# A Performer attention and mixer kernel: the second channel product by one level of Strassen's algorithm

## The chip, the cores and the metric

The kernel runs on one core of a Trainium2 chip. The metric is the device time of one execution in microseconds (us). Five engines work side by side, each through its own ordered queue: TensorE (PE in the profile; PEld is its weight loads), VectorE (DVE), ScalarE (ACT), GpSimd (POOL) and SyncE (SP, which only issues transfers). An instruction that waits holds up all that is behind it in its queue. Matrix products go to PSUM, which has eight banks of 128 x 512 fp32 values; the other engines read them from there.

## The reference

Attention with random features (8 batches, 8 heads, 576 rows, 64 columns), then one layer of an MLP mixer over the result `x` (8 x 576 x 512):

```python
q_p, k_p = (phi(q_s), phi(k_s))          # 128 features, exp
kv = np.einsum('bhsm,bhsd->bhmd', k_p, v)
num = np.einsum('bhsm,bhmd->bhsd', q_p, kv)
return (num / den)                       # becomes x, heads side by side
...
h = np.maximum(xt @ w_tok1, 0.0) @ w_tok2     # token mix, xt = x transposed
u = x + h.transpose(0, 2, 1)
h2 = np.maximum(u @ w_ch1, 0.0) @ w_ch2       # 512 -> 1536 -> 512
return (u + h2)
```

`u @ w_ch1` is the first channel product, the one with `w_ch2` the second. Inputs are fp32; the kernel computes its products in fp16 and sums in fp32.

## The kernel before

Each batch's 576 rows are split into 512 main rows and 64 tail rows. A batch goes through these stages, named by their functions:

- `attention`: per pair of heads, the feature products (L638, L652) and their exponentials on ScalarE (L514), a maximum and its reciprocal on VectorE (L664, L666), the scaling of v on GpSimd (L671), the kv product (L684), the numerators (L720, L722) and their division on VectorE (L729, L730).
- `token_mix` (`token_mix_first` for batch 0): the two token products (L759, L776), a relu between them, of whose two blocks one is on ScalarE (L765) and one on VectorE (L767), the addition that makes `u` (L779), and a transposing transfer of `u` to `uT` on SP's queue.
- `token_tail`: the tail rows of two batches at a time (L835, L841), collected as a ninth "batch" of 512 rows.
- `channel_mix(c, ...)`, for c = 0 to 7 and for c = 8, the tail rows. The first channel product (L854) makes twelve blocks of 128 channels by 512 rows, four matmuls of 512 columns each; a relu (L874, on ScalarE for batches from 2 on and all of batch 1) writes each to its place in `r3`, [128, 12, 512] fp16. The second product (L892) works through four row blocks j of 128 rows: for each, twelve matmuls with `r3`'s block as the stationary operand and `wc2[:, cb]` (512 columns) as the moving one accumulate in one bank; VectorE adds `u` and writes fp32 to `o` (L901; L898 for batch 0), and a store of 256 KB goes out from SP. `r3` has two buffers, `o` four, the PSUM banks are one ring of eight.

The order of the work isn't written by hand. Every helper registers jobs by `add` (L59): an engine, a planned cost in us, a key, what it depends on, and which ring places it takes and gives. The planner's `run` then puts them in order: for each engine it finds the jobs that can start first, with margins for work handed over between engines (0.3 us ahead of TensorE), and among those the one with the lowest key (L123, L124):

```python
first = min(r[0] for r in ready)
t, _, j = min((r for r in ready if r[0] <= first + 1e-6), key=lambda r: r[1])
```

So the order on every queue is settled when the kernel is built, from planned costs; on the chip each engine follows it and waits by semaphores. Transfers from GpSimd's queue keep the order in which they were registered. Keys come from the batch number and the tables `KEYS`, `NEAR` and `HEAD`; `BY` says which engine does some of the evacuations. Between its early jobs TensorE gets idle matmuls (L943) until the first large product.

Of the kernel before, what the change touches and what calls it, by code (L numbers as in the profile page):

```python
# [9 lines left out]
FP32 = mybir.dt.float32  # L10
FP16 = mybir.dt.float16
# [5 lines left out]
KEYS = {"a": -1.349, "as": 0.099, "t": -1.509, "ts": 0.187, "gv": 2.165, "lt": -2.428, "lv": -3.989, "to": -2.341, "tt": 0.635, "ks": 1.094, "km": 0.303, "vs": -0.113, "l1": -0.452, "kt": -0.062}  # L17
NEAR = {"1": {"a": -1.734, "as": 0.259, "t": -2.775, "ts": 0.45, "gv": -0.056, "km": -2.03, "vs": -0.397, "kt": 0.253}, "2": {"a": -2.686, "as": 0.0, "t": -0.603, "ts": 0.324, "gv": -1.313, "km": 3.931, "vs": 0.571, "lv": -3.347, "lt": -2.872, "kt": -0.122}}
HEAD = {"kp": [-3.838, -3.822, -3.881, -3.404], "ke": [-2.728, -2.927, -2.827, -2.727], "km": [-4.039, -3.592, -4.221, -2.25], "vs": [-3.448, -3.487, -3.196, -2.472], "qp": [-3.203, -3.403, -3.303, -3.488], "qe": [-3.328, -3.374, -2.153, -3.748], "kv": [-3.407, -3.257, -2.676, -3.133], "ko": [-2.32, -3.035, -3.463, -3.168], "n": [-3.199, -3.47, -3.182, -2.377, -2.999, -3.268, -2.999, -2.899], "no": [-4.124, -3.487, -3.919, -3.144, -3.226, -3.426, -3.126, -2.386], "ktm": -3.643, "kt": -4.584, "kte": -5.022, "qt": -3.759, "qte": -5.587, "kx": [-6.213, -5.658, -5.326, -5.458], "kxo": [-6.855, -7.05, -5.723, -4.783], "ktx": -5.661, "ktxo": -5.912, "qx": [-4.987, -3.488], "qxo": [-4.073, -2.977], "qtx": -4.584, "qtxo": -3.371, "t1": [0.229, -1.008, -0.737, -0.359], "re": [0.072, -0.781, 0.181, -0.024], "ut": [0.056, -0.48, -0.104, -0.341], "uo": [-0.099, -0.259, -0.108, 0.38], "vbd": -8.41, "w1": -9.7, "w1t": -9.38, "w2t": -9.78, "wa": -8.03, "wb": -9.17, "w2": -10.08}
BY = {"kx": "ADDD", "ktx": "A", "qx": "DD", "qtx": "A", "ko": "DADD", "re": "AAAA", "uo": "AADD", "no": "DDADDADD", "r0": "AAAAADAAADAA", "ko1": "DDAA", "r1": "AAAAAAAAAAAA"}  # L20
# [17 lines left out]
class Planner:  # L38
# [20 lines left out]
    def add(self, eng, cost, key, fn, deps=(), take=(), give=(), rows=False, wire=0.0):  # L59
        job = Job(eng, cost, key, fn, [d for d in deps if d is not None], list(take), list(give), rows, wire)  # L60
        for g in job.give:
            self.left[g] = self.left.get(g, 0) + 1
        self.jobs.append(job)
        return job
# [113 lines left out]
def kernel(  # L178
# [37 lines left out]
    def sb(shape, dt, name):  # L216
        return pool.tile(shape, dt, name=name)

    def ring(n, shape, dt, name):
        return [sb(shape, dt, f"{name}{i}") for i in range(n)]  # L220

    COUNT = {"qT": 3, "kT": 3, "v": 3, "vt": 2, "qp": 4, "kp": 4, "vs": 4, "qpt": 2, "kpt": 2, "vbd": 2,
             "kvsb": 3, "ktt": 2, "x": 3, "r1": 3, "u": 3, "uT": 3, "r3": 2, "o": 4, "bank": 8}
# [4 lines left out]
    omega_nat = sb([P, D], FP32, "omega_nat")  # L228
    omega16 = sb([P, 2 * D], FP16, "omega16")
    omT = sb([P, M], FP16, "omT")  # L230
    ident32 = sb([P, P], FP32, "ident32")
    ident16 = sb([P, P], FP16, "ident16")
    junk = sb([P, B], FP16, "junk")
    zeros = sb([P, SM], FP16, "zeros")
# [26 lines left out]
    t_o = ring(COUNT["o"], [P, DM], FP32, "o")  # L261
# [30 lines left out]
    def mm(n, cols):  # L292
        return n * (cols / 2400.0 + 0.0025)
# [167 lines left out]


# [289 lines left out]
    def token_mix(b, key, step, jx):  # L752
        jr = []
        for tb in range(NT):
# [7 lines left out]
            def relu(tb=tb, n=n):  # L762
                o = t_r1[place("r1", b)][:, tb, :]
                if tb == 0:
                    nc.scalar.activation(out=o, in_=bank(n), func=AF.Relu)  # L765
                else:
                    nc.vector.tensor_relu(out=o, in_=bank(n))  # L767
            jr.append(add("ACT" if tb == 0 else "DVE", 0.5 if tb == 0 else 0.69, key + step * tb * 0.2, relu, deps=[j1],
# [75 lines left out]

    def channel_mix(c, key, jt):
        def moving(db):
            return (t_uT[place("uT", c)] if c < B else uTt)[:, :, db, :]
        jr = []
        for cb in range(NCB):
# [16 lines left out]
            else:  # L866
                j1 = add("PE", mm(4, 512), key + 0.5 * cb / NCB, c1, deps=[*jt, j_wc1[cb // (NCB // 2)], *first], take=[("bank", n), ("r3", c)],
# [9 lines left out]
            jr.append(add("ACT" if on_act else "DVE", 0.5 if on_act else 0.69, key + 0.5 * cb / NCB, relu, deps=[j1], take=[("r3", c)], give=[("bank", n)]))  # L877
        for j in range(NJ):
            last = c == B and j == NJ - 1
            for hf in range(2 if last else 1):  # L880
# [15 lines left out]
                def oadd(j=j, n=n, cols=cols):  # L896
                    if c == 0:
                        nc.vector.tensor_copy(out=t_o[place("o", (c, j))], in_=bank(n))  # L898
                        return
                    uu = t_u[place("u", c)][:, j, :] if c < B else ut[j]  # L900
                    nc.vector.tensor_tensor(out=t_o[place("o", (c, j))][:, cols], in0=uu[:, cols], in1=bank(n)[:, cols], op=ALU.add)  # L901
                jo = add("DVE", (0.55, 0.27)[hf] if last else 0.69, k2, oadd, deps=[prev], take=[("o", (c, j))], give=[("bank", n)] + ([("u", c)] if 0 < c < B else []))
                def store(j=j, cols=cols, last=last):
                    o = t_o[place("o", (c, j))]
# [7 lines left out]
                dma("SP", k2, 0.65, store, deps=[jo], give=[("o", (c, j))], cost=0.4 if c < B else 0.8)  # L912
# [63 lines left out]
```

## Time and profile before

| | |
|---|---|
| median of 3 runs | 289.49 us (289.16 to 290.48) |
| profiled execution: span from first to last instruction | 287.0 us |
| profiled execution: its own time | not given beside the span; the median lies 2.5 us over the span |
| TensorE busy, mean granted clock | 280.2 us, 0.998 |
| second channel product (L892), 444 matmuls | 100.7 us |
| first channel product (L854), 424 matmuls | 99.2 us (88.7 for c below 8, 10.5 for the tail rows) |
| VectorE / ScalarE / GpSimd busy | 152.6 / 153.6 / 93.7 us |
| bytes moved by transfers | 39.59 MB, 138 GB/s on the mean |

A busy time is the union of an engine's instructions. A matmul's listed duration reaches from its start to the end of its drain, so that of two in a row overlap; the distance from start to start (the pitch) is what one costs in a stream. In a group, the number after the bar is busy us, then the mean ns of one instruction, then the idle time of the engine ahead of them with what ended it. A timeline line has start, length, engine, line, operation, tiles, shape and count.

### The profile page before, as it was taken

To read this page: it belongs to the slowest core of one execution; us is meant where nothing else is said; L and a number is where in the kernel's file an instruction comes from. 1 tells how busy PE (TensorE), PEld (TensorE's weight loads), DVE (VectorE), ACT (ScalarE), POOL (GpSimd) and SP (SyncE) were. 2 spreads that over 40 slices of the span, in tenths; PEclk is the share of its full clock that TensorE was granted. 3 is DMA by queue.
4 is the path that set the end of the run, shared out by engine and by line. 5 is a ranking of instruction groups with operands and counts; after the bars stand their busy time and mean duration, and the time that the engine had idled before them with its cause. 6 is when DMAs were issued, how large, how long until landed. Compare 5 with 4: busy or idle time off the path is not lost.

```text
span 287.0 us, 5605 instructions
## 1 busy us (share of the span) xinstructions
PE 280.2 (98%) x2186; PEld 141.6 (49%) x2186; DVE 152.6 (53%) x330; ACT 153.6 (54%) x322; POOL 93.7 (33%) x126
## 2 busy tenths in 40 slices
PE   8999999999999999999999999999999999999994
PEld 4585554445544544454445544454455444444442
DVE  3986954546669624745584647564686331031012
ACT  2984872098449552875286537753576402602600
POOL 8994950157015701480166016601141000000000
PEclk9999999999999999999999999999999999999999
DMA  8999999999975995999989967996531042013013
GB/s 191 197 191 195 202 216 143 214 196 190 166 110 149 136 175 117 202 168 198 111 156 206 201 85 144 199 189 95 129 75 39 0 110 110 2 48 116 2 45 102
DMA packets 85721, 39.59 MB, mean 138 GB/s; under 512 B 64384, under 2 KB 80128, under 8 KB 85504
## 3 DMA queue, kind: packets, MB, share of 16 engines
q0 software_dynamic: 34288, 17.45, 44.4%
q1 hardware_dynamic: 50624, 21.01, 33.2%
q10 hardware_dynamic: 784, 0.79, 0.8%
q8 instruction: 17, 0.28, 0.4%
q14 instruction: 8, 0.07, 0.1%
HBM read 35.88 MB, written 16.52 MB: 183 GB/s over the span
## 4 chain that ended last, share of the span: by engine, by line
PE 90%; POOL 5%; DMA 3%; issue 1%; ACT 0%; DVE 0%; POOLq 0%; DVEq 0%
PE bank L892 33%; PE bank L854 32%; PE bank L776 4%; PE bank L759 4%; DMA r<-in_k_dram 3%; PE bank L638 3%; PE bank L652 3%; PE bank L684 2%; PE bank L720 2%; POOL vs L671 1%; PE bank L760 1%; POOL r L313 1%; PE bank L835 1%; PE bank L485 1%; PE bank L722 1%
## 5 line engine op out<-in xcount | busy, mean ns | idle before, releaser
L892 PE MATMUL bank<-wc,r 128*128 128x512 f16 (+2 forms) x444 | 100.7, 374 | 0.0
L874 ACT ACTIVATE r<-bank 128x512 f16<-128x512 f32 x106 | 62.7, 606 | 64.5 <-PE bank L854 64.4
L854 PE MATMUL bank<-uT,wc 128*128 128x512 f16 x376 | 88.7, 379 | 0.0
L892 PEld LDWEIGHTS <-r 128*128 128x128 f16 x444 | 40.9, 98 | 48.9 <-issue 4.4
L854 PEld LDWEIGHTS <-wc 128*128 128x128 f16 x424 | 39.7, 98 | 43.1 <-issue 0.4
L514 ACT ACTIVATE qp<-bank 128x512 f16<-128x512 f32 x64 | 35.8, 646 | 13.0 <-PE bank L652 13.0
L664 DVE TENSOR_REDUCE km<-kp 128x8 f16<-128x1024 f16 x32 | 38.5, 1202 | 2.3 <-ACT kp L514 2.3
L514 ACT ACTIVATE kp<-bank 128x512 f16<-128x512 f32 x64 | 34.6, 630 | 6.6 <-PE bank L638 6.4
L671 POOL TENSOR_TENSOR vs<-v,vs 128x512 f16<-128x512 f16 x32 | 33.3, 1063 | 13.8 <-DVE vs L666 4.3
L901 DVE TENSOR_TENSOR o<-u,bank 128x512 f32<-128x512 f16 x28 | 19.1, 683 | 34.5 <-PE bank L892 34.4
L730 DVE TENSOR_TENSOR x<-bank,rc 128x320 f16<-128x320 f32 x62 | 30.5, 492 | 2.1
L779 DVE TENSOR_TENSOR u<-x,bank 128x512 f16<-128x512 f16 x28 | 17.4, 683 | 9.5 <-PE bank L776 9.5
L729 DVE RECIPROCAL rc<-bank 128x5 f32<-128x5 f32 x62 | 11.5, 186 | 16.0 <-PE bank L722 15.8
L596 POOL TENSOR_TENSOR vbd<-vt,vbd 128x512 f16<-128x512 f16 (+1 forms) x7 | 8.2, 1173 | 35.0 <-PE bank L835 14.8
L380 POOL COPY junk<-kT 128x1 f16<-128x1 f16 x6 | 1.1, 186 | 50.5 <-DMA kT<-k 50.5
L767 DVE TENSOR_SCALAR r<-bank 128x512 f16<-128x512 f32 x7 | 4.8, 692 | 21.1 <-PE bank L760 21.1
L759 PE MATMUL bank<-x,w1m 128*128 128x512 f16 x56 | 14.4, 379 | 0.0
L720 PEld LDWEIGHTS <-qp 128*128 128x128 f16 x256 | 12.3, 98 | 4.0
L684 PEld LDWEIGHTS <-kp 128*128 128x128 f16 x256 | 11.1, 98 | 5.7 <-issue 1.1
L684 PE MATMUL bank<-vs,kp 128*128 128x65 f16 x256 | 12.9, 194 | 0.7 <-ACT r L874 0.7
L720 PE MATMUL bank<-kvsb,qp 128*128 128x65 f16 x256 | 13.5, 194 | 0.0
L776 PE MATMUL bank<-r,w 128*128 128x512 f16 x56 | 13.4, 380 | 0.0
(109 smaller groups left out, 269.5 us busy)
## 6 DMA issues: line engine op xcount, KB each, us to landing
out_dram<-o SPq DMA_DIRECT2D x32, 256.0 KB, 2.7
q<-in_q_dram POOLq DMA_DIRECT2D x6, 576.0 KB, 6.8
wc<-in_moe_w_ch_dram POOLq DMA_DIRECT2D x4, 768.0 KB, 10.6
k<-in_k_dram POOLq DMA_DIRECT2D x6, 512.0 KB, 9.1
v<-in_v_dram POOLq DMA_DIRECT2D x6, 512.0 KB, 6.7
r<-in_q_dram POOLq DMA_DIRECT2D x4, 256.0 KB, 7.2
v<-in_v_dram POOLq DMA_DIRECT2D x4, 256.0 KB, 7.1
out_dram<-o SPq DMA_DIRECT2D x5, 128.0 KB, 2.3
```

The costliest lines, as they stand in the source:

```text
L514: nc.scalar.activation(out=out, in_=in_, func=AF.Exp, bias=0.0, scale=1.0)
L664: nc.vector.reduce_max(out=mx, in_=kpv, axis=AX.X)
L671: nc.gpsimd.tensor_tensor(out=vs[:, :, 0:D], in0=t_v[place("v", b)][:, hh[0] : hh[0] + 2, :].rearrange("p h (j d) -> p (h j) d", d=D), in1 ...
L684: nc.tensor.matmul(ps[:, i, :], kpv[:, 2 * i + j // 2, j % 2, :], vs[:, i * NJ + j, 0 : D + 1], start=(i == 0 and j == 0), stop=False, ski ...
L720: nc.tensor.matmul(ps[:, k, j * 65 : (j + 1) * 65], st, s[:, i, 0 : D + 1], start=True, stop=True)
L730: nc.vector.tensor_tensor(out=t_x[place("x", b)][:, :, (2 * hp + hs[0]) * D : (2 * hp + hs[0] + n) * D].rearrange("p j (i d) -> p i j d", ...
L759: nc.tensor.matmul(ps, w1m[:, j, tb * P : (tb + 1) * P], x[:, j, :], start=(j == 0), stop=False)
L776: nc.tensor.matmul(ps, w2_of(tb, j), r1[:, tb, :], start=(tb == 0), stop=(tb == NT - 1))
L854: nc.tensor.matmul(ps, wc1[:, db, cb * P : (cb + 1) * P], moving(db), start=(db == 0), stop=(db == ND - 1))
L874: nc.scalar.activation(out=o, in_=bank(n), func=AF.Relu)
L892: nc.tensor.matmul(ps[:, cols], r3[:, cb, j * P : (j + 1) * P], wc2[:, cb, cols], start=(cb == 0), stop=(cb == NCB - 1))
L901: nc.vector.tensor_tensor(out=t_o[place("o", (c, j))][:, cols], in0=uu[:, cols], in1=bank(n)[:, cols], op=ALU.add)
```

## The change

The second channel product of batches 1 to 7 is computed by one level of Strassen's algorithm in Winograd's form. `r3` (512 rows x 1536 channels) and `wc2` (1536 x 512) are cut in halves both ways, and seven products of 256 rows x 768 channels x 256 columns take the place of eight. In detail:

- Four sums of `wc2`'s quarters (T1 to T4, [128, 6, 256] fp16 each) are made once, on VectorE.
- Per batch, four sums of `r3`'s quarters (S1, S2, S3 and one that overwrites the quarter r3(1,0)) are made on VectorE in fp16, each in two halves of 128 x 768 elements: eight instructions, one after the other within a half.
- Each of the seven products is twelve matmuls with a moving operand of 256 columns. Its [256 x 256] result is one bank. Four products accumulate in bank X, two in Z, one in Y. VectorE reads bank X after each of its four products, before the next one is added to it; with one reading of Y and two of Z that makes seven readings of 128 x 512 elements a batch into `o`, which then has two buffers of two row blocks. Two stores of 512 KB take the place of four of 256 KB.
- The product waits for all twelve relus of the batch. The blocks of the first channel product are made in the order 0, 6, 1, 7, and so on.
- The second token-mix relu goes from VectorE to ScalarE (`BY["re1"]`). All of the eight sums are on VectorE (`BY["S"]` is `DDDDDDDD`).
- Four small early tiles (`zeros`, `ident32`, `omega_nat`, `omega16`) lie in the memory of `S`.
- Every job's key comes from the table `TURN`, 1195 numbers in the order of registration, divided by 1000; `KEYS["ks"]`, by which two jobs with 64-row matmuls are favoured one after the other, goes from 1.094 to 2.577.

Batch 0 and the tail rows keep the old product. The diff, without the table's numbers and the lines of `KEYS` and `BY`:

```diff
+TURN = [
...
+]
...
     def add(self, eng, cost, key, fn, deps=(), take=(), give=(), rows=False, wire=0.0):
+        key = TURN[len(self.jobs)] / 1000.0 if TURN else key
...
-             "kvsb": 3, "ktt": 2, "x": 3, "r1": 3, "u": 3, "uT": 3, "r3": 2, "o": 4, "bank": 8}
+             "kvsb": 3, "ktt": 2, "x": 3, "r1": 3, "u": 3, "uT": 3, "r3": 2, "S": 1, "o": 2, "bank": 8}
...
     banks = [pspool.tile([P, 512], FP32, name=f"bank{i}") for i in range(COUNT["bank"])]
-    omega_nat = sb([P, D], FP32, "omega_nat")
-    omega16 = sb([P, 2 * D], FP16, "omega16")
+    NH = NCB // 2
+    DH = DM // 2
+    t_S = sb([P, 3, NH, 2 * P], FP16, "S")
+    t_T = sb([P, 4, NH, DH], FP16, "T")
+    early = t_S.rearrange("p a b c -> p (a b c)")
+    zeros = early[:, 0:SM]
+    ident32 = early[:, SM : SM + 2 * P].bitcast(FP32)
+    omega_nat = early[:, SM + 2 * P : SM + 2 * P + 2 * D].bitcast(FP32)
+    omega16 = early[:, SM + 2 * P + 2 * D : SM + 2 * P + 4 * D]
...
-    ident32 = sb([P, P], FP32, "ident32")
...
-    zeros = sb([P, SM], FP16, "zeros")
...
-    t_o = ring(COUNT["o"], [P, DM], FP32, "o")
+    t_o = ring(COUNT["o"], [P, 2, DM], FP32, "o")
...
+    W11, W12, W21, W22 = [wc2[:, NH * i : NH * i + NH, DH * e : DH * e + DH] for i in range(2) for e in range(2)]
+    T1, T2, T3, T4 = [t_T[:, i] for i in range(4)]
+    j_T = []
+    for out_, a, b in ((T1, W12, W11), (T2, W22, T1), (T3, W22, W12), (T4, W21, T2)):
+        j_T.append(add("DVE", 0.95, KEYS["T"], lambda o=out_, a=a, b=b: nc.vector.tensor_tensor(out=o, in0=a, in1=b, op=ALU.subtract), deps=[*j_wc2, *j_T[-1:]]))
...
             j1 = add("PE", mm(5, 512), key + step * tb * 0.2, t1, deps=[*jx, j_w1, j_w1t[b % 2]], take=[("bank", n), ("r1", b)])
...
-                if tb == 0:
+                if tb == 0 or BY["re1"] == "A":
                     nc.scalar.activation(out=o, in_=bank(n), func=AF.Relu)
...
-            jr.append(add("ACT" if tb == 0 else "DVE", 0.5 if tb == 0 else 0.69, key + step * tb * 0.2, relu, deps=[j1],
+            on_act = tb == 0 or BY["re1"] == "A"
+            jr.append(add("ACT" if on_act else "DVE", 0.5 if on_act else 0.69, key + step * tb * 0.2, relu, deps=[j1],
...
+    def channel_out_fast(c, key, jr):
+        def r3(i, e):
+            return t_r3[place("r3", c)][:, NH * e : NH * e + NH, 2 * P * i : 2 * P * i + 2 * P]
+        def S(i):
+            return t_S[:, i - 1]
+        sums = {}
+        for g in range(2):
+            part = slice(g * NH // 2, (g + 1) * NH // 2)
+            need = [jr[cb + NH * e] for cb in range(part.start, part.stop) for e in range(2)]
+            steps = (
+                (1, lambda: (S(1), r3(1, 0), r3(1, 1)), ALU.add),
+                (3, lambda: (r3(1, 0), r3(0, 0), r3(1, 0)), ALU.subtract),
+                (2, lambda: (S(2), S(1), r3(0, 0)), ALU.subtract),
+                (4, lambda: (S(3), r3(0, 1), S(2)), ALU.subtract),
+            )
+            prev = []
+            for k, (i, what, op) in enumerate(steps):
+                on_pool = BY["S"][4 * g + k] == "P"
+                def go(what=what, op=op, part=part, on_pool=on_pool):
+                    o, a, b = what()
+                    (nc.gpsimd if on_pool else nc.vector).tensor_tensor(out=o[:, part], in0=a[:, part], in1=b[:, part], op=op)
+                job = add("POOL" if on_pool else "DVE", 1.6 if on_pool else 0.5, key + KEYS["S"] + 0.1 * g + 0.01 * k, go, deps=[*need, *prev], take=[("S", c)])
+                prev = [job]
+                sums.setdefault(i, []).append(job)
+        last = sums[4]
+        ops = (
+            ("X", lambda: r3(0, 0), W11, []),
+            ("Y", lambda: r3(0, 1), W21, []),
+            ("X", lambda: S(2), T2, last),
+            ("Z", lambda: S(1), T1, last),
+            ("X", lambda: r3(1, 0), T3, last),
+            ("Z", lambda: S(3), W22, last),
+            ("X", lambda: r3(1, 1), T4, last),
+        )
+        ends = {"X": 6, "Y": 1, "Z": 5}
+        step = (1.0 - KEYS["c2"]) / 7
+        held = {}
+        def read(k, b, i, e, base, deps, free):
+            def go():
+                o = t_o[place("o", (c, i))][:, :, DH * e : DH * e + DH]
+                ps = bank((b, c)).rearrange("p (j d) -> p j d", j=2)
+                a = t_u[place("u", c)][:, 2 * i : 2 * i + 2, DH * e : DH * e + DH] if base else o
+                nc.vector.tensor_tensor(out=o, in0=a, in1=ps, op=ALU.add)
+            return add("DVE", 0.69, key + KEYS["c2"] + step * k, go, deps=deps, take=[("o", (c, i))],
+                       give=([("bank", (b, c))] if free else []) + ([("u", c)] if base else []))
+        done, outs = [], {}
+        for k, (b, a_of, w, need) in enumerate(ops):
+            def go(k=k, b=b, a_of=a_of, w=w):
+                ps, a = bank((b, c)), a_of()
+                for j in range(2):
+                    for cb in range(NH):
+                        nc.tensor.matmul(ps[:, j * DH : (j + 1) * DH], a[:, cb, j * P : (j + 1) * P], w[:, cb, :],
+                                         start=(b not in held and j == 0 and cb == 0), stop=False, skip_group_check=True)
+                held[b] = True
+            deps = [*need, *jr, *j_T, *j_wc2] + ([outs["sA"]] if k == 2 else [outs["s2"]] if k == 4 else [outs["22"]] if k == 5 else [outs["s3"]] if k == 6 else [])
+            j = add("PE", mm(2 * NH, DH), key + KEYS["c2"] + step * k, go, deps=deps, take=[("bank", (b, c))], give=[("r3", c)] + ([("S", c)] if need else []))
+            j.heavy = True
+            if k == 0:
+                outs["sA"] = read(k, "X", 0, 0, True, [j], False)
+            elif k == 1:
+                outs["11"] = read(k, "Y", 0, 0, False, [j, outs["sA"]], True)
+            elif k == 2:
+                outs["s2"] = read(k, "X", 0, 1, True, [j], False)
+            elif k == 3:
+                j_z = j
+            elif k == 4:
+                outs["s3"] = read(k, "X", 1, 1, True, [j], False)
+                outs["22"] = read(k + 0.1, "Z", 1, 1, False, [j_z, outs["s3"]], False)
+            elif k == 5:
+                outs["12"] = read(k, "Z", 0, 1, False, [j, outs["s2"]], True)
+            else:
+                outs["21"] = read(k, "X", 1, 0, True, [j], True)
+        for i, need in ((0, ["11", "12"]), (1, ["21", "22"])):
+            def store(i=i):
+                nc.sync.dma_start(out=out[c, 0:SM, :].rearrange("(p j) d -> p j d", j=NJ)[:, 2 * i : 2 * i + 2, :], in_=t_o[place("o", (c, i))])
+            dma("SP", key + 0.9 + 0.1 * i, 1.3, store, deps=[outs[x] for x in need], give=[("o", (c, i))], cost=0.4)
     def channel_mix(c, key, jt):
         def moving(db):
             return (t_uT[place("uT", c)] if c < B else uTt)[:, :, db, :]
-        jr = []
-        for cb in range(NCB):
+        jr = [None] * NCB
+        fast = NPE - 1 <= c < B
+        order = [x for i in range(NH) for x in (i, i + NH)] if fast else range(NCB)
+        for pos, cb in enumerate(order):
...
-                j1 = add("PE", mm(4, 512), key + 0.5 * cb / NCB, c1, deps=[*jt, j_wc1[cb // (NCB // 2)], *first], take=[("bank", n), ("r3", c)],
+                j1 = add("PE", mm(4, 512), key + 0.5 * pos / NCB, c1, deps=[*jt, j_wc1[cb // (NCB // 2)], *first], take=[("bank", n), ("r3", c)],
                        give=[("uT", c)] if c < B else [])
             j1.heavy = True
...
-            jr.append(add("ACT" if on_act else "DVE", 0.5 if on_act else 0.69, key + 0.5 * cb / NCB, relu, deps=[j1], take=[("r3", c)], give=[("bank", n)]))
+            jr[cb] = (add("ACT" if on_act else "DVE", 0.5 if on_act else 0.69, key + 0.5 * pos / NCB, relu, deps=[j1], take=[("r3", c)], give=[("bank", n)]))
+        if fast:
+            channel_out_fast(c, key, jr)
+            return
         for j in range(NJ):
...
                 k2 = key + 0.5 + 0.5 * (3 * j + 3) / 12
                 def oadd(j=j, n=n, cols=cols):
                     if c == 0:
-                        nc.vector.tensor_copy(out=t_o[place("o", (c, j))], in_=bank(n))
+                        nc.vector.tensor_copy(out=t_o[place("o", (c, j // 2))][:, j % 2], in_=bank(n))
                         return
                     uu = t_u[place("u", c)][:, j, :] if c < B else ut[j]
-                    nc.vector.tensor_tensor(out=t_o[place("o", (c, j))][:, cols], in0=uu[:, cols], in1=bank(n)[:, cols], op=ALU.add)
-                jo = add("DVE", (0.55, 0.27)[hf] if last else 0.69, k2, oadd, deps=[prev], take=[("o", (c, j))], give=[("bank", n)] + ([("u", c)] if 0 < c < B else []))
+                    nc.vector.tensor_tensor(out=t_o[place("o", (c, j // 2))][:, j % 2, cols], in0=uu[:, cols], in1=bank(n)[:, cols], op=ALU.add)
+                jo = add("DVE", (0.55, 0.27)[hf] if last else 0.69, k2, oadd, deps=[prev], take=[("o", (c, j // 2))], give=[("bank", n)] + ([("u", c)] if 0 < c < B else []))
                 def store(j=j, cols=cols, last=last):
-                    o = t_o[place("o", (c, j))]
+                    o = t_o[place("o", (c, j // 2))][:, j % 2]
...
-                dma("SP", k2, 0.65, store, deps=[jo], give=[("o", (c, j))], cost=0.4 if c < B else 0.8)
+                dma("SP", k2, 0.65, store, deps=[jo], give=[("o", (c, j // 2))], cost=0.4 if c < B else 0.8)
...
```

## The prediction

> **What bounds the kernel now.** I read the profile in this order: the page's busy table and its chain, a window that leaves out start and end, the timeline of TensorE, then that of the engines it hands to. The page first.
>
> ```profile
> span 287.0 us, 5605 instructions
> PE 280.2 (98%) x2186; PEld 141.6 (49%) x2186; DVE 152.6 (53%) x330; ACT 153.6 (54%) x322; POOL 93.7 (33%) x126
> PEclk9999999999999999999999999999999999999999
> PE 90%; POOL 5%; DMA 3%; issue 1%; ACT 0%; DVE 0%; POOLq 0%; DVEq 0%
> ```
>
> TensorE is the chain, at full granted clock. The window from 44 to 284 us, in the columns PE, PEld, DVE, ACT, POOL, then clock, DMA share and GB/s:
>
> ```profile
> 44.00:284.00 240.00, 238.90 (x1727) 116.05 (x1723) 120.86 (x247) 122.36 (x248) 58.94 (x78) 1.00 0.72 128
> ```
>
> 1.1 us of 240 is not PE, and that is what follows the last matmul at the end. So time is TensorE's instruction stream, added up. Its timeline gives the pitch (a listed length contains the last matmul's drain, so I use differences of starts):
>
> ```profile
> 20.26 0.39 PE L803 MATMUL bank<-x,w1m 128*128 128x128 f16 x4
> 20.49 0.22 PE L804 MATMUL bank<-x,w1t 128*128 128x128 f16 x1
> 20.54 0.39 PE L803 MATMUL bank<-x,w1m 128*128 128x128 f16 x4
> ...
> 230.24 10.52 PE L892 MATMUL bank<-wc,r 128*128 128x512 f16 x48
> 240.60 10.52 PE L854 MATMUL bank<-uT,wc 128*128 128x512 f16 x48
> 250.96 3.62 PE L892 MATMUL bank<-wc,r 128*128 128x512 f16 x16
> ```
>
> 48 matmuls of 512 columns take 10.36 us, 215.8 ns each; five of 128 columns take 0.28 us, 56 ns each, every one with its own weight load. Between them (215.8 - 56)/384 = 0.416 ns a column.
>
> The VectorE timeline at the end of a block, and the groups by shape:
>
> ```profile
> 233.03 0.69 DVE L901 TENSOR_TENSOR o<-u,bank 128x512 f32<-128x512 f16 x1 [2.27 <-PE bank L892]
> ...
> L671 POOL TENSOR_TENSOR vs<-v,vs 128x512 f16<-128x512 f16 x32 | 33.3, 1063 | 13.8 <-DVE vs L666 4.3 <-PE bank L722 3.6 <-PE bank L684 2.4
> L730 DVE TENSOR_TENSOR x<-bank,rc 128x320 f16<-128x320 f32 x62 | 30.5, 492 | 2.1
> L901 DVE TENSOR_TENSOR o<-u,bank 128x512 f32<-128x512 f16 x28 | 19.1, 683 | 34.5 <-PE bank L892 34.4
> L492 DVE COPY qT<-bank 128x1024 f16<-128x1024 f16 x4 | 2.6, 660 | 0.0
> L492 DVE CAST kT<-bank 128x512 f16<-128x512 f32 x3 | 2.0, 688 | 2.3 <-PE bank L485 2.2
> ```
>
> The first quarter of L892's 48 matmuls ends at 230.24 + 12 x 0.2158 = 232.83, and L901 begins at 233.03: 0.2 us from the last matmul to the reader, then 0.69 us of reading. VectorE is at 120.86/240 = 50%, and TensorE waits for it nowhere here.
>
> **The change, part by part.** *Products.* Batches 1 to 7 lose 48 matmuls of 512 columns each, 10.36 us. They get 7 products of 12 matmuls at 256 columns. That shape isn't in the trace, so I take the line between its neighbours: 56 + 128 x 0.416 = 109.3 ns, bounded by 107.9 (half of 215.8) and 112 (twice 56). 84 x 109.3 = 9.18 us. The gain is 1.18 us a batch, 8.3 us for seven (6.7 to 9.1 by the two bounds).
>
> Weight loads nearly double, from 48 to 84 a batch; at 128 columns a load per matmul already hides in 56 ns, so I cost them nothing; uncovered they would have raised that pitch first. The Trainium skill, "TensorE: Matmul & The Clock Gate", section "Back-to-back issue gap", speaks against the change: it gives streams of load and matmul about 81 ns at 128 columns and 131 ns at 512. By these, 256 columns would be an estimated 98 ns, a batch would go from 48 x 131 = 6.3 to 84 x 98 = 8.2 us, and the kernel would lose some 14 us. This case's rows are 56 and 215.8 ns, and they decide.
>
> *Sums of activations, on VectorE.* Eight per batch, 128x768, all operands fp16. L492 moves 1024 fp16 elements in 660 ns and 512 fp32 in 688, so fp16 costs half as much per element there: 768 such elements are 0.40 + 0.13 = 0.53 us. The other end is the rate of two-input L901: 768/512 x (683 - 150) + 150 = 0.95 us. I take 0.53, since every long two-input VectorE row in the trace has a 32-bit operand, and here none has. 8 x 0.53 = 4.2 us a batch, or 7.6. The four weight sums (1536 elements, 0.93 or 1.75 us each) come once, 3.7 or 7 us, in the middle of the kernel's first half, where VectorE is half idle.
>
> *Readings.* Seven additions of 128x512 in place of four, 0.683 each: 2.05 us a batch more. One token-mix relu, 0.69 us, goes from VectorE to ScalarE. VectorE's new load from 44 us on is 120.9 + 7 x (4.2 + 2.05 - 0.69) + 3.7 = 164 us in a window that shrinks to about 232: 71%, up from 50. ScalarE goes to 126.6, 55%. Neither is the bound on the mean.
>
> *New waits on TensorE.* The running bank X is read between products, so product 3 waits for the first reading, 5 for the second, and 6 and 7 for the third (6 also for the reading of Z after it). In TensorE's ordered queue, everything behind a late product waits as well. A reading is 0.2 + 0.69 = 0.9 us from the last matmul. Products 2 and 4 (1.31 us each) cover the first two. After product 5 nothing of the same batch covers: 0.9 us, and 1.5 where 6 is put before 7. At the front, product 1 needs all twelve relus: 0.2 + 0.6 (L874) = 0.8 us after the batch's last L854 matmul. Product 3 needs the chain of sums after that relu: 4 x 0.53 = 2.1 us plus handing over, against 2.6 us of products 1 and 2. Uncovered, all this is some 2.3 us a batch, 16 us in seven; at the least it is nothing. The cover is other work that TensorE has between two batches: a batch takes some 29 us, of which this product is 9, and for the last batch it is L854's 10.4 us on the tail rows. The row nearest to it is the window above: by the same planner, with its margins, TensorE stood for nothing in 240 us, though every kv and every relu is such a handover. VectorE being fuller makes lateness likelier, so I take 1.0 us in all, with 0 and 16 as ends.
>
> *Contention.* No long two-input VectorE row in SBUF exists in the trace. GpSimd is busy with L671 and its like for 4 x 1.06 + 1.05 = 5.3 us of each batch's 29. The Trainium skill, "SBUF — State Buffer", section "Who interferes with whom", says that a VectorE instruction with both inputs in SBUF and a GpSimd instruction that reads SBUF shut each other out for a whole instruction; no run here shows it. Should they block, the sums would come at most 5.3 us later in a batch, by the row, off TensorE's path while its other work lasts; I price it inside the 0 to 16.
>
> *Stores.* Fourteen stores of 512 KB replace 28 of 256 KB on SP's queue, each waiting for two readings; the transposes queued behind on SP (uT, 4.5 us to landing) wait with them. The last ones, of the tail rows, stay, so the end after the last matmul stays near 4 us. Cost nothing; if a transpose is late, the wait appears at L854's counterpart.
>
> *Order table.* It replaces every key. In the first 24 us TensorE waits for loads, and a different order there can give or take what one block costs: 0 taken, -1.5 to +1.5. The same holds for the switch between 64-row and 128-row matmuls (each adds some 0.1 us in the timeline): 0 taken, -2 to +2.
>
> *Sum.* The profiled execution spans 287.0 us. It isn't timed by itself; the median of the runs, 289.5, is 2.5 us over its span, and I take these to lie around it. 289.5 - 8.3 + 1.0 = 282.2 us.
>
> **The rivals.**
> *A: half the gain goes into waits.* The uncovered 0.9 us after product 5 is paid in about half the batches, and a late sum in others: 4 to 6 us back, 285 to 288. For it: 71% VectorE in order. Against it: 19 us of other work a batch.
> *B: no change.* Waits of 1.18 us a batch eat exactly the gain: 288 to 291.
> *C: slower, by the waits at bank X and at the sums.* From 1.18 us of uncovered wait a batch the change loses. With the sums at 0.95 us, the chain is 3.8 us against 2.6 of cover, and VectorE's load rises by 24 + 3 us to 191 of 232, 82%; up to 2.3 + 1.2 = 3.5 us a batch then gives 289.5 - 8.3 + 24 = 305. For it: the planner's table holds costs, not measured times, and nothing in the trace shows this fp16 addition. Against it: that lateness must outlast the cover in nearly every batch.
> *D: a better start.* The table also takes 2 to 3 us out of the first 24 us and the switches: 277 to 279.
>
> **How the numbers follow.** The forecast with its own range 279 to 285 (the sum with its start, switch and pitch ends and up to 4 us of waits): 0.70. A 0.10, B 0.05, C 0.12, D 0.03. About 0.5%, 1.4 us, can be told from no change. Faster is the forecast, A and D, 0.83; same B, 0.05; slower C, 0.12. The range that holds eight in ten takes in A: 279 to 288.
>
> **What would show it.** Right: TensorE's busy time falls by about 8 us with no idle time from 44 us on, the 256-column pitch is near 109 ns, the sums take some 0.53 us, and the chain stays nine tenths TensorE. A pitch of 125 ns or more would undo the gain by itself (84 x 123 = 10.36). Wrong: idle time of TensorE ended by VectorE at the products' line; sums near 0.95 us or stretched beside L671; VectorE in the chain; L854 waiting for uT; or a first L854 that comes later than at 26.8 us.

## The result and the profile after

The changed kernel has a median of 288.77 us over 20 runs (283.99 to 295.43), against 289.01 us (288.58 to 290.78) for 20 runs of the kernel before. The ratio is 0.9914 with an interval of 0.9888 to 0.9941; it is taken over the runs within 1.5% of each kernel's fastest, and that leaves out the eleven longest of the changed kernel, whose scatter turns out below to be its own late transfers and not a disturbed chip. The forecast was 282.2 us, with a range of 279.0 to 288.0. By the medians the whole gain of 7 us is missing, and the median lies outside the range; by the ratio (0.9914 x 289.0 = 286.5 us) some 4 us of it are.

The profiled execution after took 290.0 us, 1.8 us more than its span; it is one of the longer runs, and so shows the loss well. Its page, in the lines shown of before:

```profile
span 288.2 us, 6125 instructions
PE 274.5 (95%) x2438; PEld 166.0 (58%) x2438; DVE 192.6 (67%) x404; ACT 158.5 (55%) x329; POOL 93.2 (32%) x126
PEclk9999999999999999999999999999799999999999
PE 74%; DMA 14%; DVE 4%; POOL 3%; ACT 2%; issue 1%; POOLq 0%; DVEq 0%; SPq 0%
```

TensorE works 5.7 us less than before, and yet the span is 1.2 us longer. The chain has gone from 3% to 14% of DMA, and one slice of the forty has a lower clock. Three rows of the view of TensorE's waits after (engine and line, what it waited for: total us, times, longest):

```profile
PE bank L740 <- DMA qT<-q: 5.3, 1, 5.3
PE bank L772 <- POOL vs L759: 1.3, 2, 1.1
...
PE bank L1025 <- DMA uT<-u: 0.4, 1, 0.4
```

One stop of 5.3 us, for the transposed q of batch 7. No wait at the products (L988) for VectorE is on the list. The timeline of TensorE after, around that stop:

```profile
197.29 1.03 PE L865 MATMUL bank<-r,w 128*128 128x512 f16 x4
203.66 1.04 PE L740 MATMUL bank<-qT,omT 64*128 64x512 f16 x4 [5.34 <-DMA qT<-q]
204.63 1.90 PE L865 MATMUL bank<-r,w 128*128 128x512 f16 x4
206.32 1.83 PE L988 MATMUL bank<-T,S 128*128 128x256 f16 x12
208.09 0.29 PE L634 MATMUL bank<-omT,kT 64*128 64x128 f16 x4
```

Four matmuls of L865 take 1.03 us before the stop and 1.90 after it. From the first L740 to L634 it is 4.43 us. In a run without the stop (experiment 4 below) the same stretch takes 2.83:

```profile
197.28 0.60 PE L740 MATMUL bank<-qT,omT 64*128 64x512 f16 x4
...
200.11 0.29 PE L634 MATMUL bank<-omT,kT 64*128 64x128 f16 x4
```

So the stop costs 5.3 us of standing and 1.6 us of half speed, 6.9 in all: 288.2 - 6.9 = 281.3 us of span.

What the stop waited for stands in the chain of waits after, between 165 and 212 us, in order of time (start, us, what):

```profile
170.29 9.28 DMA uT<-u
179.62 2.76 PE bank L1025 x12
...
187.30 16.32 DMA qT<-q
203.62 0.04 issue
203.66 1.04 PE bank L740 x4
```

A transposing transfer that takes 4.9 to 9.2 us in the kernel before took 16.3. The timeline of SP's queue after shows its neighbours (start, us on the queue, line and transfer):

```profile
170.29 4.89 SPq L873 DMA_TRANSPOSE uT<-u  x1
181.06 2.32 SPq L1011 DMA_DIRECT2D out_dram<-o  x2
184.78 1.46 SPq L932 DMA_TRANSPOSE uTt<-ut  x1
187.30 9.40 SPq L456 DMA_TRANSPOSE qT<-q  x1
```

And GpSimd's queue after, in the same stretch:

```profile
179.70 0.19 POOL L468 COPY junk<-uT 128x1 f16<-128x1 f16 x1 [3.00 <-DMA uT<-u]
180.18 0.57 POOL L435 DMA_DIRECT2D q<-in_q_dram  x1 [0.29 <-issue]
180.74 1.70 POOL L446 DMA_DIRECT2D k<-in_k_dram  x2
```

The loads of batch 7's q and k go out at 180.2 to 182.4 us, as soon as uT of batch 5 has landed (L468 reads it), and two stores of 512 KB go out at 181.06 and 183.05, in the middle of them. In the kernel before the same loads go out at 176.1, qT has landed at 193.0 (8.5 us after its issue), and its first use is at 202.9: 10 us of slack. The lines of GpSimd's, SP's and TensorE's timelines before:

```profile
176.07 0.57 POOL L353 DMA_DIRECT2D q<-in_q_dram  x1
...
184.52 4.32 SPq L374 DMA_TRANSPOSE qT<-q  x1
...
202.86 0.38 PE L652 MATMUL bank<-qT,omT 64*128 64x512 f16 x2
```

After, even a run without the stop (experiment 4) has qT at 192.2 us and uses it at 197.3, because TensorE is 5 us further: 5 us of slack. The lag begins earlier: before, a load of v went out at 165.1 us and had landed at 171.0, when uT was just starting; after, it goes out at 169.6, behind a kT that landed at 169.5 instead of 164.9, and shares its time with uT, which takes 9.3 us instead of 4.3.

What the forecast didn't look at is in the window from 40 to 200 us (columns PE, PEld, DVE, ACT, POOL, clock, DMA share, GB/s). Before:

```profile
40.00:200.00 160.00, 160.00 (x1277) 79.35 (x1276) 95.64 (x205) 92.38 (x193) 53.67 (x73) 1.00 0.98 163
```

After:

```profile
40.00:200.00 160.00, 157.52 (x1444) 94.82 (x1442) 124.00 (x257) 96.25 (x199) 52.41 (x72) 1.00 1.03 154
```

In the kernel before, the DMA share was already 0.98 in the stretch where most loads, transposing transfers and stores lie. (The share adds up packet times and can pass one, as the 1.03 shows; so 0.98 is a high load, but not a proven ceiling.) The window shown with the forecast has 0.72, because it runs on to 284 us, over 80 us with a share of 0.24.

Four theories then. *Late transfers*: the products, the sums and the table do what was forecast, and what is missing is batch 7's q (or a neighbour) coming late. *Engines*: VectorE's extra load costs the time, and transfers only show it. *The 512 KB stores*: they alone delay the transfer. *The table*: the new order alone costs the time.

### The profile page after: what moved, and what is told of

Its sections match the earlier page's. It is cut to its first block, busy times and chain, and to the rows that moved or that the text cites. A ratio compares the mean times of both kernels' runs of the same rounds, so it can differ in the third digit from the quotient of the medians.

```text
span 288.2 us, 6125 instructions
## 1 busy us (share of the span) xinstructions
PE 274.5 (95%) x2438; PEld 166.0 (58%) x2438; DVE 192.6 (67%) x404; ACT 158.5 (55%) x329; POOL 93.2 (32%) x126
## 4 chain that ended last, share of the span: by engine, by line
PE 74%; DMA 14%; DVE 4%; POOL 3%; ACT 2%; issue 1%; POOLq 0%; DVEq 0%; SPq 0%
PE bank L1025 28%; PE bank L988 20%; PE bank L1066 6%; DMA qT<-q 6%; PE bank L865 4%; PE bank L847 4%; DMA uT<-u 3%; DMA r<-in_k_dram 3%; PE bank L772 2%; PE bank L808 2%; DMA v<-in_v_dram 2%; PE bank L740 2%; PE bank L726 2%; DVE km L752 2%; POOL vs L759 1%
## 5 line engine op out<-in xcount | busy, mean ns | idle before, releaser
L1025 PEld LDWEIGHTS <-wc 128*128 128x128 f16 x424 | 39.1, 98 | 41.9 <-issue 1.9
L988 PEld LDWEIGHTS <-r 128*128 128x128 f16 x336 | 32.1, 98 | 7.6 <-issue 1.5
L988 PEld LDWEIGHTS <-S 128*128 128x128 f16 x252 | 24.0, 99 | 6.4 <-issue 1.8
L1066 PE MATMUL bank<-wc,r 128*128 128x512 f16 (+2 forms) x108 | 22.9, 356 | 0.0
L988 PE MATMUL bank<-T,S 128*128 128x256 f16 x168 | 21.1, 276 | 0.0
L988 PE MATMUL bank<-T,r 128*128 128x256 f16 x168 | 20.7, 273 | 0.0
L988 PE MATMUL bank<-wc,r 128*128 128x256 f16 x168 | 20.7, 273 | 0.0
L978 DVE TENSOR_TENSOR o<-o,bank 128x512 f32<-128x512 f32 x21 | 14.2, 676 | 7.8 <-PE bank L988 6.8
L602 ACT ACTIVATE qpt<-bank 128x256 f16<-128x256 f32 x16 | 7.0, 484 | 19.8 <-PE bank L699 19.8
L740 PE MATMUL bank<-qT,omT 64*128 64x512 f16 x64 | 11.9, 395 | 5.3 <-DMA qT<-q 5.3
```

The lines of the kernel that those rows point to most:

```text
L602: nc.scalar.activation(out=out, in_=in_, func=AF.Exp, bias=0.0, scale=1.0)
L740: nc.tensor.matmul(ps[e], omT[half[e]], t[half[e], 2 * hp : 2 * hp + 2, 0:R], start=True, stop=True)
L978: nc.vector.tensor_tensor(out=o, in0=a, in1=ps, op=ALU.add)
L988: nc.tensor.matmul(ps[:, j * DH : (j + 1) * DH], a[:, cb, j * P : (j + 1) * P], w[:, cb, :], start=(b not in held and j == 0 and cb == 0), ...
L1025: nc.tensor.matmul(ps, wc1[:, db, cb * P : (cb + 1) * P], moving(db), start=(db == 0), stop=(db == ND - 1))
L1066: nc.tensor.matmul(ps[:, cols], r3[:, cb, j * P : (j + 1) * P], wc2[:, cb, cols], start=(cb == 0), stop=(cb == NCB - 1))
```

## The experiments

The first four stand against a median of 288.96 us of before on the same chip, the next four against 288.73, the last two against 288.76. Each number of an experiment is a median.

**1. Light loads.** For batches 3 to 7 the loads of q and k bring 64 columns instead of all, and the transposing transfers read batch 2's scratch; so the loading of those q and k is left out and everything else stays.

```diff
-                    out=scratch[w, b].rearrange("(p r) e -> p (r e)", p=P),
+                    out=scratch[w, b].rearrange("(p r) e -> p (r e)", p=P)[:, 0 : 64 if b > 2 else H * S * D // P],
...
-                nc.sync.dma_start_transpose(out=t.unsqueeze(1), in_=scratch[w, b])
+                nc.sync.dma_start_transpose(out=t.unsqueeze(1), in_=scratch[w, min(b, 2)])
```

> The order of every engine is that of the changed kernel. The loads of q and k of batches 3 to 7 into their fp16 copies move a few per cent of their bytes, and the transposing transfers of these batches read batch 2's copies instead: the loading of q and k of batches 3 to 7 is left out of the computation. Theory (late transfers: TensorE stands for batch 7's qT at 198 us because q, k, v loads, 512 KB stores and transposes crowd each other, and loses about 7 us there with the cold clock behind it; the sizes of the products and sums were right): 281 to 283 us, no stop of TensorE over 1 us after 44 us, and the runs lie within 1 us of each other. Rival (engines: VectorE too full, sums shut out by GpSimd): the time stays at 286 to 290 with the same scatter, since no engine has less to do.

Measured: 281.91 us (281.67 to 282.41), ratio 0.9751 [0.9729, 0.9774], span 280.6. The window of this kernel, same columns:

```profile
40.00:200.00 160.00, 159.88 (x1471) 96.54 (x1470) 125.28 (x260) 98.49 (x205) 51.44 (x74) 1.00 0.72 127
```

VectorE is as full as after, 125 of 160 us, and TensorE stands for 0.12 us of 160. With the DMA share at 0.72 the forecast time is there. The theory of the engines falls: nothing was taken from VectorE, ScalarE or GpSimd's arithmetic.

**2. An older q.** Batch 7's features of q are taken from the buffer of batch 6, which is long there. Batch 7's q isn't used then.

```diff
-        t = (t_qT if w == "q" else t_kT)[place(w + "T", b)]
+        t = (t_qT if w == "q" else t_kT)[place(w + "T", 6 if b == 7 and w == "q" else b)]
```

> Batch 7's q features are made from batch 6's transposed q, so that TensorE doesn't wait for batch 7's (its own q is left out of the computation); every transfer still runs. Theory of late transfers, if batch 7's q is the one late transfer: 282 to 284. If its k, landing 2 to 3 us after q, or transfers of other batches are late as well in many executions: 284 to 287, with idle time of TensorE moved to kT or uT. Engines as the cause: no change, 286 to 290.

Measured: 286.41 us (284.05 to 287.3), ratio 0.9896 [0.9858, 0.9933]; faster than after by the medians, but not by the whole, and the two ratios' intervals overlap. The stop went elsewhere. The timeline of TensorE in this kernel:

```profile
152.99 0.60 PE L772 MATMUL bank<-vs,kp 128*128 128x65 f16 x8 [2.25 <-POOL vs L759]
```

and the chain of this kernel just before it:

```profile
141.07 9.64 DMA v<-in_v_dram
...
151.89 1.06 POOL vs L759
152.95 0.04 issue
152.99 0.60 PE bank L772 x8
```

Here v of batch 5 was late: issued at 141.1 beside a uT at 141.3, landed at 150.7, with no store in flight (the next goes out at 150.5). So it isn't one transfer that is late, and GpSimd, which the wait names, only passes the lateness on (its own 1.06 us is unchanged).

**3. Keys in place of the table.** All of the change, with the keys of before and its new ones.

```diff
-        key = TURN[len(self.jobs)] / 1000.0 if TURN else key
+        key = key
```

> The changed kernel without its table: every job's key is again the one of its stage, with the seven products, the sums and the rest as in the change. If the table's order is what brings TensorE to batch 7's q too early: 282 to 285 and a smaller scatter. If the table earns something over the keys: 286 to 293, with more idle time of TensorE than the 8 us of the changed kernel's profile.

Measured: 284.08 us (283.93 to 284.46), ratio 0.9826 [0.9804, 0.9848]. The Strassen product in the old manner of ordering is 1.7% faster than before, and its runs agree within 0.5 us, where those of after scatter over 11. In its profile the loads of batch 7's q and k go out at 178.0 to 180.3 us and the two stores at 184.6, behind them. In the median the table costs 4.7 us, by the two ratios 2.5.

**4. No stores in batches 3 to 5.** Of each 512 KB store of these batches only 64 columns of one row block are written, so their storing is left out.

```diff
-                nc.sync.dma_start(out=out[c, 0:SM, :].rearrange("(p j) d -> p j d", j=NJ)[:, 2 * i : 2 * i + 2, :], in_=t_o[place("o", (c, i))])
+                nc.sync.dma_start(out=out[c, 0:SM, :].rearrange("(p j) d -> p j d", j=NJ)[:, 2 * i : 2 * i + 2, :], in_=t_o[place("o", (c, i))]) if not 3 <= c <= 5 else nc.sync.dma_start(out=out[c, 0:SM, :].rearrange("(p j) d -> p j d", j=NJ)[:, 2 * i, 0:64], in_=t_o[place("o", (c, i))][:, 0, 0:64])
```

> The stores of batches 3, 4 and 5 move 1/16 of a row block each in place of 512 KB (the storing of their results is left out). If the two stores of 512 KB issued at 181 us are what holds up batch 7's k and q (loads that took 12 to 19 us to land where they took 6 to 9 in the kernel before): 282 to 284, and qT lands within 10 us of its issue. If it is the order of loads and transposes among themselves: 285 to 289, and qT still takes over 12 us in slow executions.

Measured: 282.16 us, ratio 0.9777 [0.974, 0.9814]. Four of six runs took 282.0 to 282.2 and two 285.2 and 286.9. In its profile, qT of batch 7 landed 6.5 us after its issue instead of 16.3. Taking the stores away brings the forecast in most runs, not in all: the stores are the usual last straw, not the only one. It isn't a clean test of the store beside the loads alone: with fewer stores uT of batch 5 lands sooner too, and the loads of q go out at 177.0 us instead of 180.2.

**5 and 6. The stores later in SP's order.** All work is done; the two stores of a batch c (1 to 4) are issued behind a transposing transfer of batch c + 3, the one of k (experiment 5) or the one of q (experiment 6). The diff of experiment 5; the other has q in place of k in its second line:

```diff
-            j.fn()
+            j.fn() if j.late is None or j.late.done else self.parked.setdefault(id(j.late), []).append(j.fn); j.done = True; [f() for f in self.parked.pop(id(j), [])]
...
+            ld[w + "T", b] = dma("SP", key + 0.2 + 0.01 * n, 2.2, back, deps=casts, take=[(w + "T", b)], cost=2.5); [setattr(stores[b - 3, i], "late", ld["kT", b]) for i in range(2) if w == "k" and (b - 3, i) in stores]
```

> All engines as in the changed kernel, all work done; only on SP's queue the two 512 KB stores of batches 1 to 4 are issued behind the transposing transfers of q and k three batches on, in place of ahead of them. If the stores, issued within 2 us of the loads of q and k, are what holds those up: 282 to 284, with most runs within 1 us, and q and k of batch 7 land by 196 us. If the 84% of DMA time is simply too much whatever the order: the stores now hold up uT and v in place of q, and the time stays at 285 to 290 with its scatter. Engines as the cause: no change.

> As the last, but the stores go between the transposes of q and k. Stores against loads as the cause: 282.5 to 286, since k's transposed copy waits behind 1 MB of stores (some 5 us) and has 5 to 6 us of slack in an undisturbed execution. Too much transfer in any order: 285 to 290.

Measured: 283.75 us (283.65 to 283.89), ratio 0.9822 [0.9805, 0.9839], for the first, and 282.68 us (282.15 to 283.88), ratio 0.9792 [0.9769, 0.9814], for the second. SP's queue in experiment 6:

```profile
170.97 2.33 SPq L873 DMA_TRANSPOSE uT<-u  x1
185.01 1.20 SPq L932 DMA_TRANSPOSE uTt<-ut  x1
186.32 4.67 SPq L456 DMA_TRANSPOSE qT<-q  x1
191.04 1.05 SPq L1011 DMA_DIRECT2D out_dram<-o  x2
```

and its window:

```profile
40.00:200.00 160.00, 159.88 (x1469) 96.44 (x1469) 125.08 (x260) 98.44 (x205) 54.24 (x74) 1.00 0.99 161
```

The same transfers, a share of 0.99, and no stop: it is which transfer stands beside which that decides, not their sum. Experiment 5 has no late transfer either, but pays a new wait. Its timeline of VectorE:

```profile
110.82 0.69 DVE L978 TENSOR_TENSOR o<-u,bank 128x512 f32<-128x512 f16 x1 [2.12 <-DMA out_dram<-o]
```

There are two `o` buffers; a store that is held back keeps one of them, the first reading waits for it, and the next product waits for the reading (0.94 us of TensorE at 111.56).

**7. Keys and light loads.** Experiments 1 and 3 together, to see whether the order by keys also loses to transfers.

> The kernel without the table (284.1 us), with the loads of q and k of batches 3 to 7 cut to a few per cent (that loading is left out of the computation). If the keys' order loses its 2 us against the undisturbed table's 281.9 in waits between engines: 283 to 284, little changed. If it loses them to transfers as well: 281.5 to 282.5, and the table earns nothing.

Measured: 283.81 us (283.46 to 283.96), ratio 0.9821 [0.9803, 0.9839], the same as with keys alone. From 44 to 200 us TensorE stands for 1.04 us there, against 0.12 us under the table with light loads, mostly at ScalarE (0.7 us) and GpSimd (0.2); another 0.7 us is at VectorE later. So the table is worth 2 us (281.9 against 283.8) if its transfers come in time, and costs 2.5 to 4.7 if they don't.

**8. Earlier loads.** The GpSimd instruction that the loads stand behind reads u, not uT; so the loads of q and k no longer wait for uT's landing. All work is done.

```diff
-            nc.gpsimd.tensor_copy(out=junk[:, b : b + 1], in_=t_uT[place("uT", b)][:, NJ - 1, ND - 1, P - 1 : P])
+            nc.gpsimd.tensor_copy(out=junk[:, b : b + 1], in_=t_u[place("u", b)][:, NJ - 1, DM - 1 : DM])
```

> All work done, orders as in the changed kernel; but the loads of q and k of a batch are let go when the u of two batches before is made, not when its transposed copy has landed (some 4 to 9 us earlier). If it is the late start of these loads that makes them late: 282 to 285. If the crowd of transfers is the cause, they now run against the transposes of u, which TensorE needs first: 286 to 292, with TensorE waiting for uT.

Measured: 282.81 us (282.15 to 284.27), ratio 0.9794 [0.9768, 0.982]. The loads of batch 7's q go out at 177.6 us instead of 180.2, only 2.6 us earlier, since GpSimd has other work in front of them; that is enough to be ahead of the stores, which go out at 181.9.

**9. Both cures.** Experiments 6 and 8 together.

> All work done; stores of batches 1 to 4 between the transposes of q and k, and loads of q and k let go at u. Each alone gave 282.7 and 282.8 us. If what is left in them is still a late transfer now and then (282.2 to 284.3 among their runs): 282 to 282.7 with a smaller scatter. If nothing is left to late transfers: 282.3 to 283, the same. If the two get in each other's way (the earlier loads run against u's transposes, and the stores push k's further back): 283.5 to 286.

Measured: 282.41 us (281.9 to 283.87), ratio 0.9779 [0.9757, 0.9802]: not told apart from either cure alone. Its profile has one wait for a transfer left from 44 us on, for uT of batch 5, at 179 us:

```profile
PE bank L1025 <- DMA uT<-u: 1.7, 1, 1.7
```

**10. The changed kernel again**, on the chip of experiment 9, with no edit.

> The changed kernel once more, on the same chip as the last, for comparison. If its scatter comes from its own transfers: a median of 286 to 290 and a spread of 4 us or more, beside the other kernels' 1 to 2. If it came from the chip on which it was first timed: 282 to 284.

Measured: 288.72 us (286.12 to 291.66, 13 runs), ratio 0.9947 [0.9927, 0.9967]. TensorE's waits in this execution:

```profile
PE bank L772 <- POOL vs L759: 5.5, 3, 4.2
PE bank L740 <- DMA qT<-q: 2.4, 1, 2.4
```

In this run batch 7's v is late as well as its q (13.6 us for qT). The scatter belongs to the kernel, not to a chip: 17 runs of before on this chip lie within 1.3 us. Which transfer is late differs between the three profiled executions with a stop: qT (after), v (experiment 2), v and qT (here).

## Why the prediction was wrong

**The base.** The forecast put 2.5 us around the span. The runs of before are 2.0 us over theirs, so its profiled execution took about 289.0, not 289.5. 0.5 us.

**Products: right.** The timeline of TensorE after, late in the span:

```profile
270.08 1.47 PE L988 MATMUL bank<-T,r 128*128 128x256 f16 x12
271.39 1.89 PE L1025 MATMUL bank<-uTt,wc 128*128 128x512 f16 x8
```

1.31/12 = 109.2 ns at 256 columns with a weight load each, forecast 109.3. So the 8.3 us are there, and the weight loads cost nothing. The Trainium skill, "TensorE: Matmul & The Clock Gate", section "Back-to-back issue gap", has figures for sustained streams (not the formula that it gives for an isolated matmul) that would have put this shape near an estimated 98 ns and 512 columns at 131, where the runs show 109.2 and 215.8; trusting the rows over these figures was right.

**Sums and readings: right.** The groups by shape after (busy us, mean ns, idle before):

```profile
L978 DVE TENSOR_TENSOR o<-u,bank 128x512 f32<-128x512 f16 x28 | 19.0, 678 | 15.2 <-PE bank L988 15.1
...
L955 DVE TENSOR_TENSOR S<-r,S 128x768 f16<-128x768 f16 x14 | 7.8, 555 | 0.3
...
L955 DVE TENSOR_TENSOR S<-S,r 128x768 f16<-128x768 f16 x14 | 7.7, 551 | 0.0
```

0.55 us a sum (forecast 0.53, other end 0.95) and 0.68 a reading. No row shown gives the fixed 0.13 us in the 0.53; without it the row of L492 scales to 0.50. The load on VectorE is 124 of 160 us, 78%, in the stretch where the loads lie.

**New waits on TensorE: smaller than forecast.** Of the 1.0 us (bounds 0 and 16), 0.12 us was left between 44 and 200 us in experiments 1, 4, 6 and 8. VectorE at 78%, in order, makes TensorE late nowhere in these four. Rival C, the waits at bank X and at the sums, is not what happened, nor is A: each has its place at L988, and there only experiment 5, by its held-back store, and the order by keys (0.7 us) show a wait.

**Contention on GpSimd's side: no cost.** None of the 56 sums overlaps a GpSimd operation in the profile after. The Trainium skill, "SBUF — State Buffer", section "Who interferes with whom", names a second way: a VectorE instruction can hold up a DMA that GpSimd issues, by starving GpSimd while it writes the descriptors; but the page found this for copies and not for tensor_tensor, the operation of these sums. For batch 7's loads the sums are excluded by time as well: they were issued from 180.2 to 184.2 us and the next sum began at 193.1, and experiments 4, 6 and 8 have their sums within 1 us of the same place.

**Order table: the sign depends on the transfers.** Costed at 0 (-1.5 to +1.5). It is worth 2 us between the engines (experiment 7 against 1) and costs 4.7 us in the median with the real transfers (experiment 3 against after). A table fixes an order of issue; it was costed as if only TensorE's order were in it.

**Stores: the step that failed.** The prediction says "Cost nothing; if a transpose is late, the wait appears at L854's counterpart." It named the mechanism, the stores that the transposing transfers stand behind, but priced it at nothing and looked for it at uT only. It measured 6.9 us in the profiled execution (5.3 of standing, 1.6 of half speed), at L740 behind qT, and 0.4 us at uT. It gave no reason for the nothing, and compared no landing with its first use: TensorE arrives 5 us earlier, and half of the slack of 10 us is gone. Experiments 1 (fewer bytes), 4 (fewer stores), 6 (stores behind) and 8 (loads in front) each brought 281.9 to 282.8 us. The step is wider than the stores: in experiment 2 a v came late beside a uT alone. And it is not the share by itself: with 0.98 to 0.99 from 40 to 200 us, TensorE stands for 0.12 us from 44 to 200 us in experiments 4, 6 and 8.

**The sum, redone.** 289.0 - 8.3 + 0.1 = 280.8 would be the time if nothing else were lost; the runs without a late transfer take 282 to 283 by their medians. In the profile of experiment 6 the difference lies in three places: TensorE stands 0.75 us more in the first 44 us (40.58 busy against 41.33), which is inside the bounds given for the start, 0.45 us more after 200 us (4.56 against 4.11), and its work is 272.8 us where 280.2 - 8.3 = 271.9. What sets these three isn't settled. That the forecast agrees with experiments 1, 4 and 9 to 0.3 us owes something to a base 0.5 us too high and waits 0.9 us too high, which these losses happened to balance. A run of the changed kernel is then 282 us plus what it loses to late transfers, 2 to 13 us.

**Rival B (no change) has the median, and rival A (285 to 288) the 286.5 us of the ratio, but neither by its mechanism**: both eat the gain with waits at the products or sums, B a steady 1.18 us a batch. What ate it in the profiled executions is one or a few waits for transfers, at a batch that TensorE reaches too soon.

**What stays open.** Why one transposing transfer takes 16.3 us beside loads and stores, and 6.5 without the stores or with the stores behind it, is shown only by its neighbours, not by its inside. The size of the stores wasn't varied by itself: in the kernel before, four of 256 KB go out from 173.5 to 184.1 us beside the same loads, and qT lands in 8.5 us. And experiment 9 with 1.7 us at uT says that the slack is thin still.

## What to carry to other kernels

When the bound of a kernel is made faster, look at the share of every other resource in the stretch where that resource is used, not over the whole span: 0.72 over 240 us hid 0.98 over 160. A high share is a reason to look and not a verdict, for experiment 6 keeps 0.99 and has no late transfer. Then take the time of each use and the time of each landing, and ask which landing is nearest: here 10 us of slack became 5, and one transfer 11 us late took 6.9 of the 8.3 us that seven batches had gained. An order that is better for the engines is to be judged with its transfers; the stores of four batches, each pair moved behind one transfer, gave back 6 us.

## What the runs showed of the hardware

- A transposing transfer slows strongly beside loads through GpSimd's queue and large stores: uT takes 4.3 us at best and 9.3 beside a v load, qT 6.3 to 16.3 us in one execution after. The Trainium skill, "DMA: Bandwidth & Descriptors", section "Issuing engines are not separate DMA queues", says that transfers from all issuing engines run on the same 16 DMA engines and interleave there; the runs agree, and add by how much one can be stretched.
- A stop of TensorE costs more than its length. After 5.3 us the granted clock was 0.51 from 203.6 to 207.1 us, and matmuls of 512 columns started 427 ns apart instead of 215.8; in experiment 2, after a stop of only 2.25 us, it was 0.59 from 153 to 157 us. The Trainium skill, "TensorE: Matmul & The Clock Gate", section "Part 1: The HAM clock gate (the "warmup" mystery)", says that the clock falls to a half after an idle window of about 3.4 us; the stop of 5.3 us agrees, and with the one of 2.25 us a shorter one was enough. The price of one such drop was 1.6 us.
- VectorE and GpSimd slowed each other where they met, in experiment 3. The Trainium skill, "SBUF — State Buffer", section "Who interferes with whom", speaks of an exclusive lock; the runs show such an effect, at a small price. The timeline of VectorE in that kernel:

```profile
142.57 0.55 DVE L955 TENSOR_TENSOR S<-S,r 128x768 f16<-128x768 f16 x1
143.04 0.68 DVE L978 TENSOR_TENSOR o<-u,bank 128x512 f32<-128x512 f16 x1
143.63 0.81 DVE L955 TENSOR_TENSOR S<-r,S 128x768 f16<-128x768 f16 x1
```

beside GpSimd in the same kernel:

```profile
142.82 1.21 POOL L684 TENSOR_TENSOR vbd<-vt,vbd 128x512 f16<-128x512 f16 x1 [3.04 <-PE bank L988]
```

The sum that began during GpSimd's instruction took 0.81 us instead of 0.55 and ended 0.41 us after it; GpSimd's took 1.21 instead of 1.05. The sum's 0.26 us is less than the 0.40 us for which the two records overlap, so that a lock for the whole instruction isn't shown. Five of the 56 sums meet a long GpSimd instruction in that profile: two take 0.26 us more, one 0.04, and two nothing.
